# Attention, 2D FFT and a ReLU MLP on one core: the written-out order of the work made anew from the last loads of w2 on, with some of the w2 product's helper sums on GpSimd

## The chip, the core and the metric

One core of one Trainium2 chip runs the whole kernel. TensorE (PE in the profile), VectorE (DVE), ScalarE (ACT), GpSimd (POOL) and SyncE (SP) each work through their own list of instructions in order and wait on semaphores for each other and for DMAs. The metric is device time in microseconds (us), the median of the timed runs; lower is better.

## The reference

```python
scores = scale * np.matmul(q, k.transpose(0, 1, 3, 2))
...
keep = is_global | is_local          # 8 global keys, 96 local ones
...
scores = np.where(keep, scores, -1000000000.0)
a = np.exp(scores - max); a = a / (sum + 1e-09)
x = np.matmul(a, v)                  # as (4, 768, 512)
...
u = x + np.real(np.fft.fft(np.fft.fft(x, axis=1), axis=2))
un = (u - mu) / np.sqrt(var + 1e-06)
ch = np.maximum(un @ w_ch1, 0.0) @ w_ch2
return u + ch
```

There are 4 batches of 768 rows, 8 heads of 64, and a model width of 512; w_ch1 is 512 x 2048, w_ch2 is 2048 x 512. The bias of the scores falls with the distance between query and key (ALiBi), and makes most of a row's keys vanish.

## The kernel before

**Stages.** A batch goes through attention (scores, exponential on ACT, product with the mask table on DVE, product with v), is written to DRAM as xd by ACT's queue (`wr` in `bounce`, L872/L874) and read back with other rows on the partitions as xr: four sixths by SP's queue (`rd`, L884), two sixths by an indirect DMA from POOL in reversed order (`rg`, L887). The FFT uses the symmetry of the real part: DVE folds the sequence, PE multiplies with tables (py, then pu), ACT or DVE evict (zy, L1118/L1120), a reversed copy rev is made (L1139 to L1141), and DVE adds pu to xr, which gives u and its sums (L1232 to L1251). Then the rows are normed (un, L1269/L1271), turned by a DMA transpose on SP's queue into unT (L1292), and go through the MLP.

**Chunks.** The 3072 rows make 12 chunks of 256 rows, three to a batch. A chunk has eight ph units (eight matmuls of 128 x 256 each, evicted with ReLU into hT by ACT L1344 or DVE L1345) and its products with w2. Chunks 0 and 1 take eight pg units (L1370). Chunks 2 to 11 use a scheme with seven half products instead of eight: p1, p6 and p7 add up in one PSUM tile, pgA, and p4+p5 and p3+p2 in another, pgD (L1484); DVE adds them to u (L1502). The scheme needs four sums of blocks of hT for each chunk, each 128 x 1024 in fp16, made by `s_sums`: s1 (L1448) and s2 (L1454) in tiles that p45 and p6 read, s3 (L1451) in place in hT, and s4 (L1459) over s2 when p6 is done, for the product that reads it last. It needs sums of w2's blocks as well (`w2_sums`, L1420 to L1426), which DVE makes once, in two halves; the second to fourth sums overwrite w2 and so wait until the products of chunks 0 and 1 are done. All of the sums are on DVE.

**What sets the order.** `Plan` holds, for each engine, a table `ORDER` with the names of its work in the order of issue, and `run` issues each engine's next name at the time that a planner's costs give. The costs decide only how the engines' lists interleave in the program's text and which ring buffer a unit takes; each engine's own order is the table's. In the names A is an attention unit (A45 to A56 are the scores of the third batch, batch 2, A57 to A60 its products with v, A61 to A76 the same of batch 3), M a unit of the FFT or the norm, H a ph unit (H8c to H8c+7 belong to chunk c), G a product with w2 (G0 to G15 for chunks 0 and 1, G16+5(c-2) and the four after it for chunk c). A name with a dot is an operation that follows that PE unit, and T.n is one of the others: the xd writes, the sums, the transposes, the stores.

Of the kernel before, what the change touches and what calls it, by code (L numbers as in the profile page):

```python
# [12 lines left out]
ALU = mybir.AluOpType  # L13
# [11 lines left out]
class Plan:  # L25
# [9 lines left out]
    MIX = 1.3  # L35
    LANDED = {"HW": 0.55, "SW": 1.3}
    LAT = {"ACT": 0.14, "DVE": 0.12, "POOL": 0.08}
# [84 lines left out]
    def op_go(self, eng, name, start):  # L122
# [6 lines left out]
        if eng == "POOL":  # L129
            self.ports.append((start, end, 1 if dma else 0 if outs and outs[0][0] in ("vB", "kB") else 2))  # L130
        if dma:
            at = max(max(end + 0.55, 5.5) if eng == "POOL" else end + lat + 2.7 * (lat == 1.0 and end > 3.5), self.now)
# [19 lines left out]

    SHARED = {"kB": 1, "vB": 1, "sid": 1, "f1": 0, "f2": 0, "f3": 0, "z": 0, "g0": 0, "w": 0, "s": 0, "w2a": 0, "w2t": 0, "ex": 0}
# [3 lines left out]
    def beside(self, start, cost, kind):  # L157
# [4 lines left out]
        if names:  # L162
            s = self.op_start("POOL", names[-1])
            if s is not None:
                p = self.made[names[-1]]
                ports = ports + [(max(s, start), max(s, start) + p[0]["POOL"][0], 1 if p[7] else 0 if p[3] and p[3][0][0] in ("vB", "kB") else 2)]
# [15 lines left out]
    def move(self, go=False):  # L182
# [4 lines left out]
        both = [h[2] for k, h in act if k != "AQ" or sw]  # L187
        each = sum(both) * (self.MIX if len(both) > 1 else 1.0) / 1000.0
        rate = {k: h[2] / 1000.0 if k == "AQ" and not sw else each for k, h in act}
        t = min([self.now + h[1] * rate[k] for k, h in act] + [h[0] for k, h in heads if h[0] > self.now + 1e-9] + [self.NEVER])  # L190
        if not go:
            return t
# [28 lines left out]
    def unit_start(self, unit):  # L221
# [7 lines left out]
        if not there:  # L229
# [126 lines left out]
def pool(n):  # L356
    return 0.16 + n / 1080.0


@with_exitstack  # L360
def kernel(
# [156 lines left out]
    def load_v(b, hp):  # L518
        h0 = 2 * hp
        if b >= FB:  # L520
# [3 lines left out]
            swq(whole, 1.08, [("avdone", b - 2), ("wl", 7)], [("v", b, hp, t) for t in range(2)], (1536, 0.93), False)  # L524
            return
        if b == 1:
            for t in range(2 - hp % 2 * 2):
# [3 lines left out]
                swq(four, 1.08, [], [("v", b, hp, t), ("v", b, hp + 1, t)], (1536, 0.93))  # L531
            return
        for t in range(2):
# [3 lines left out]
            swq(run, 0.85, ([("avdone", b - 2), ("wl", 7)] if b > 1 else []), [("v", b, hp, t)], (768, 0.93), b < 2)  # L537
# [4 lines left out]
    def load_qk(b, hp):  # L542
# [3 lines left out]
        for w, src in enumerate((q, k)):  # L546
            if b >= FB:
                for h in range(2):
# [4 lines left out]
                    swq(run, 0.85, free(tag, ti) + [("wl", 7)], [("qk", n, w, h)], (768, 0.93), False)  # L553
# [25 lines left out]
            if n == 4:  # L579
# [5 lines left out]
                swq(two, 1.08, free(tag, ti), [("qk", n, w), ("qk", n + 1, w)], (1536, 1.53))  # L585
# [7 lines left out]
            swq(run, 0.85, free(tag, ti), [("qk", n, w)], (768, 1.53))  # L593
# [110 lines left out]
    def score(b, hp, g):  # L704
# [3 lines left out]
        def run(start, ring):  # L708
# [37 lines left out]
            e = pl.pe((0.45, 0.45, 0.34)[g] if pem else 0.24, start, "64x64" if pem else "64x32")  # L746
# [61 lines left out]
    def av(b, hp):  # L808
# [28 lines left out]
        def part(start, ring, x, k):  # L837
# [15 lines left out]
            pl.later([("DVE", 0.17 + 0.03 * m + m * dve(384), lambda: norm(po, k))], free(*XT[b]), e,  # L853
# [10 lines left out]
    def bounce(b):  # L864
# [26 lines left out]
        pl.later([("POOL", 1.1, rg)], xw + [("xr", b), ("c", "back")], 0.0, [("xg", b)], dma=(128, 4.94), rank=0)  # L891

    def fold_s(b):
# [3 lines left out]
        for n, (c0, cw) in enumerate(parts):  # L897
# [43 lines left out]
            pl.later([("DVE", (4 if b else 2) * dve2(cw), f3)], [("f2", b, n)], 0.0, [("f3", b, n)])  # L941
# [192 lines left out]
    def mirror(b):  # L1134
# [8 lines left out]
        pl.later([("POOL", 0.8, lambda: r0(nc.gpsimd.tensor_copy)), ("DVE", 0.3, lambda: r0(V.tensor_copy))], [("y", b, 0, 3), ("y", b, 3, 3)] + free("rev0", b), 0.0,  # L1143
# [286 lines left out]
    def s_sums(c):  # L1430
# [16 lines left out]
        def s1():  # L1447
            VT(new(0), block(1, 0), block(1, 1), op=ALU.add)  # L1448
# [340 lines left out]
```

## Time and profile before

| what | value |
|---|---|
| timed runs (3) | 246.86, 248.51, 248.96 us, median 248.51 |
| profiled execution, its own time | 245.87 us |
| its span, first to last instruction | 244.1 us |
| mean granted TensorE clock | 0.991 |
| DMA traffic | 32.85 MB, mean 135 GB/s |

The profile gives one execution. The page's first part is the busy time of each engine; the table by stages gives it for stretches of the span, with the number of instructions in brackets; the timeline lists instructions with their start, their length and, in brackets, the idle time ahead of them with what ended it; the chain of waits follows the end of the span back to what released each step. Matmuls overlap, so the distance from one PE unit's start to the next (its pitch) is shorter than the length that a row gives: 0.87 us for a ph unit, of which the row says 1.04.

### The profile page before, as it was taken

The page shows a single profiled execution, that of the slowest core. Times are in us where ns is not written, and L with a number is a line of the kernel's source. Part 1 is how long each engine was busy: PE and PEld are TensorE (multiplying, and loading weights), DVE is VectorE, ACT ScalarE, POOL GpSimd, SP SyncE. Part 2 cuts the span into 40 slices and gives each one's busy share as a digit, 9 for nine tenths or more (in the row PEclk, how much of TensorE's full clock was granted, in tenths as well). Part 3 has the DMA queues.
Part 4 walks back from the last instruction along what each step waited for, and adds up shares of the span by engine and source line. Part 5 has one row for each costly group of instructions (what it writes and reads, how often), then busy time and mean ns, then how long its engine had stood idle before and what let it go on. Part 6 is the DMA issues. An engine that isn't in the chain of part 4 may idle for free.

```text
span 244.1 us, 7606 instructions
## 1 busy us (share of the span) xinstructions
PE 232.0 (95%) x3251; PEld 191.2 (78%) x3251; DVE 193.4 (79%) x420; ACT 138.8 (57%) x226; POOL 114.8 (47%) x164
## 2 busy tenths in 40 slices
PE   7679899999999999999999999999999999999993
PEld 2557776878677667788989888898889898888883
DVE  2559997879972789999999889889998755846483
ACT  2368788864657468658357788364534651434200
POOL 8998898866590038999059056500300320011020
PEclk9997999999999999999999999999999999999999
DMA  6999999999999999999999979220570330040212
GB/s 170 181 169 145 157 235 172 197 190 196 110 145 152 234 179 205 117 135 110 242 184 285 135 84 156 46 33 13 174 258 4 77 99 0 1 130 1 89 72 99
DMA packets 95938, 32.85 MB, mean 135 GB/s; under 512 B 84160, under 2 KB 92480, under 8 KB 95904
## 3 DMA queue, kind: packets, MB, share of 16 engines
q0 software_dynamic: 66176, 17.06, 71.7%
q1 hardware_dynamic: 26560, 12.56, 25.1%
q10 hardware_dynamic: 3168, 2.75, 4.1%
q8 instruction: 25, 0.41, 0.7%
q14 instruction: 9, 0.07, 0.1%
HBM read 31.44 MB, written 8.65 MB: 164 GB/s over the span
## 4 chain that ended last, share of the span: by engine, by line
PE 67%; DMA 14%; DVE 5%; ACT 5%; POOL 3%; issue 3%; SPq 1%; POOLq 0%
PE ph L1339 29%; PE pgD L1484 14%; PE pgA L1484 10%; DMA qk<-in_q_dram 4%; DMA v<-in_v_dram 4%; PE py L1105 3%; DMA hT<-in_q_dram 3%; PE pg L1370 3%; PE pav L822 3%; ACT ex L766 2%; DMA back<-backm 2%; DMA xr<-xd,back 2%; PE sc L737 2%; PE pu L1192 1%; ACT mk L1657 1%
## 5 line engine op out<-in xcount | busy, mean ns | idle before, releaser
L1339 PE MATMUL ph<-unT,w 128*128 128x256 f16 x768 | 94.4, 273 | 0.8 <-issue 0.4
L1339 PEld LDWEIGHTS <-w 128*128 128x128 f16 x768 | 73.6, 98 | 12.5 <-issue 1.2
L1344 ACT ACTIVATE hT<-ph 128x512 f16<-128x512 f32 x73 | 42.9, 596 | 54.6 <-PE ph L1339 52.6
L1484 PEld LDWEIGHTS <-hT 128*128 128x128 f16 x320 | 31.0, 98 | 4.3 <-issue 0.4
L1285 POOL TENSOR_SCALAR sm<-sm 128x2 f32<-128x2 f32 x12 | 3.4, 284 | 58.2 <-ACT un L1278 57.8
L763 ACT ACTIVATE er<-sc 128x1024 f16<-128x1024 f32 (+1 forms) x24 | 22.3, 951 | 11.4 <-PE sc L737 8.2
L1345 DVE TENSOR_SCALAR hT<-ph 128x512 f16<-128x512 f32 x23 | 15.7, 687 | 12.7 <-PE ph L1339 12.7
L766 ACT ACTIVATE ex<-sc 128x1024 f16<-128x1024 f32 (+1 forms) x24 | 21.7, 955 | 7.1 <-PE sc L743 6.9
L1502 DVE SCALAR_TENSOR_TENSOR u<-pgA,sm,u 128x256 f32<-128x256 f32 (+1 forms) x30 | 16.9, 568 | 6.4 <-PE pgA L1484 6.0
L1502 DVE SCALAR_TENSOR_TENSOR u<-pgD,sm,u 128x512 f32<-128x512 f32 (+1 forms) x21 | 15.2, 722 | 3.5 <-PE pgD L1484 3.3
L1355 POOL DMA_INDIRECT out_dram<-u,back x4 | 4.5, 1120 | 27.5 <-DVE rev L1140 16.3
L887 POOL DMA_INDIRECT xr<-xd,back x3 | 4.8, 1602 | 25.4 <-PE pg L1370 16.1
L1370 PE MATMUL pg<-w,hT 128*128 128x512 f16 x64 | 16.0, 379 | 0.0
L1118 ACT ACTIVATE zy<-py 128x1024 f16<-128x1024 f32 (+1 forms) x13 | 11.1, 857 | 8.4 <-PE py L1105 6.1
L778 DVE TENSOR_TENSOR ex<-er,mk 128x1024 f16<-128x1024 f16 (+1 forms) x24 | 15.1, 646 | 0.7 <-ACT er L763 0.7
L1278 ACT ACTIVATE un<-un 128x512 f16<-128x512 f16 x24 | 15.0, 625 | 1.1 <-DMA unT<-un 1.1
L552 POOL DMA_DIRECT2D qk<-in_k_dram x16 | 13.7, 903 | 1.2 <-DMA w<-in_moe_w_ch_dram 0.8
L1269 ACT ACTIVATE un<-u,sm 128x512 f16<-128x512 f32 x19 | 13.1, 717 | 1.9 <-DVE sm L1251 0.7
L552 POOL DMA_DIRECT2D qk<-in_q_dram x16 | 13.6, 870 | 0.0
L822 PEld LDWEIGHTS <-ex 128*128 128x128 f16 x352 | 12.4, 97 | 1.1 <-ACT ex L766 0.4
L834 DVE TENSOR_TENSOR x<-pav,rc 128x384 f16<-128x384 f32 x24 | 12.6, 554 | 0.6
L822 PE MATMUL pav<-v,ex 128*128 128x65 f16 x224 | 12.9, 193 | 0.2
(170 smaller groups left out, 492.9 us busy)
## 6 DMA issues: line engine op xcount, KB each, us to landing
w<-in_moe_w_ch_dram POOLq DMA_DIRECT2D x8, 512.0 KB, 13.4
out_dram<-u SPq DMA_DIRECT2D x15, 256.0 KB, 3.0
v<-in_v_dram POOLq DMA_DIRECT2D x12, 192.0 KB, 5.8
qk<-in_k_dram POOLq DMA_DIRECT2D x16, 96.0 KB, 5.4
qk<-in_q_dram POOLq DMA_DIRECT2D x16, 96.0 KB, 4.5
xr<-xd SPq DMA_DIRECT2D x3, 512.0 KB, 4.6
xd<-x ACTq DMA_DIRECT2D x2, 768.0 KB, 4.5
v<-in_v_dram POOLq DMA_DIRECT2D x8, 96.0 KB, 7.0
```

Source lines behind the costliest of these rows:

```text
L552: nc.gpsimd.dma_start(qk16[n][:, w, :, h], src[b, h0 + h].rearrange("(i m) d -> m i d", m=P))
L763: A(mine(), cut(pa), AF.Exp, 0.0, 0.125)
L766: A(cut(expst[hp][:, :, g * 512:g * 512 + (384 if g == 2 else 512)]), cut(pa), AF.Exp, 0.0, 0.125)
L778: VT(o, mine(), m, op=ALU.mult)
L822: nc.tensor.matmul(o[:, s * 65:(s + 1) * 65], lhsT, w, start=(a == 0), stop=(a == len(ops) - 1), skip_group_check=True)
L1278: A(x, x, AF.Square, accum_out=MV[c][:, a, 2:3])
L1339: nc.tensor.matmul(ph[:, a * CH:(a + 1) * CH].rearrange("p (x m) -> p x m", x=2), W1[0][:, d, jb * P:(jb + 1) * P], UNT[c][:, :, d, :], st ...
L1344: pl.later([("ACT", act(512), lambda: A(dst, ph, AF.Relu)), ("DVE", dve(512), lambda: V.tensor_scalar_max(dst, ph, 0.0))], [], e, [("h", c ...
L1345: ("DVE", dve(512), lambda: V.tensor_scalar_max(dst, ph, 0.0))],
L1370: nc.tensor.matmul(pg, HT[c][:, jb, t * P:(t + 1) * P], W2[0][:, jb, :], start=(jb == 0), stop=(jb == NJ - 1))
L1484: nc.tensor.matmul(o, lhs(j), rhs(j), start=(first and j == 0), stop=(j == NK - 1), skip_group_check=True)
L1502: V.scalar_tensor_tensor(o, x, r(t), acc, op0=ALU.mult, op1=ALU.add)
```

## The change

The tables' beginnings are kept: on PE up to H12, the unit that starts at 57.45 us in the trace of before, on the other engines to about the same time. Behind it every table is made anew. The planner's costs are changed at many places, which acts only through what is said above of them. Three of the edits change what the engines do:

- The sums s1 to s4 of chunks 3 to 11 may stand in POOL's table as well as in DVE's (`slow`). In the new tables 14 of the 40 are on POOL: s2 and s3 of chunk 3, s4 of chunk 4, s1 of chunk 5, s1, s2, s3 of chunk 6, s2, s3, s4 of chunk 7, s1 and s3 of chunk 9, s2 of chunk 10 and s2 of chunk 11. In exchange two of the four vB copies of batch 2 and one of batch 3 (L793/L795) and batch 2's rev go from POOL to DVE, and batch 3's rev from DVE to POOL.
- PE does the same units in another order. Two score groups of batch 2 that stood behind G20 (A48, A49) stand ahead of G17, and the first product of chunk 3, G21, stands behind the last of chunk 4's ph units in the list, H39, where it stood among the first of them.
- ACT writes batch 1's xd earlier in its list, and SP's read of it stands one place earlier; SP's later stores and POOL's loads are reordered: chunk 1's rstd on POOL (M8.8), which stood ahead of eight loads of batch 2's q and k, stands behind them.

Lines below H12 move by 11 to 14 in the changed kernel (s1 is L1459, s3 L1462, s2 L1465, s4 L1470). The edits, without the planner's other costs, and one line of the tables for each of PE, DVE and POOL:

```diff
+def pool2(n):
+    return 0.2 + n / 450.0
...
-        def s1():
-            VT(new(0), block(1, 0), block(1, 1), op=ALU.add)
+        def s1(on=V):
+            on.tensor_tensor(new(0), block(1, 0), block(1, 1), op=ALU.add)
...
+        def slow(fn):
+            return [("POOL", pool2(NK * P), lambda: fn(nc.gpsimd))] if c > 2 else []
+
-        pl.later([("DVE", us, s1)], hs + sfree(0), 0.0, [("s", c, 1)], rank=1)
+        pl.later([("DVE", us, s1)] + slow(s1), hs + sfree(0), 0.0, [("s", c, 1)], rank=1)
...
-            "H26 H27 G17 A56 A50 H31 G18 A55 M20 G19 A57 H28 H30 A60 H29 G20 A48 A49 H32 H33 A59 G21 A58 H36 H38 G22 G23 H34 G24 H37 H39 G25 H35 A61 A62 "
+            "H29 G18 A53 A56 H31 H30 A54 A50 H28 G19 M20 G20 A55 A52 H24 H26 A58 H39 G21 A59 A57 G22 A60 H37 H32 G23 H38 H36 G25 G24 H33 H34 A61 A72 H35 "
...
-            "A56.1 A50.1 G18.0 M17.7 G17.0 M20.0 A55.1 T.203 A57.0 A60.0 G19.0 G20.0 T.207 T.208 A48.1 A49.1 A59.0 T.210 A58.0 G21.0 T.142 G23.0 T.209 "
+            "T.126 A56.1 T.124 A53.1 G17.0 T.123 M20.0 A50.1 G19.0 A54.1 G20.0 A52.1 T.207 A58.0 A55.1 A57.0 G21.0 A59.0 A60.0 G22.0 G23.0 T.209 T.142 "
...
-            "T.112 T.158 T.163 T.167 T.125 T.126 T.169 T.164 T.156 T.153 T.154 T.124 T.162 T.155 M17.5 T.141 M17.11 T.157 T.166 T.172 T.160 T.159 M20.5 "
+            "G15.1 T.169 T.125 T.162 T.163 T.159 M17.5 T.166 T.155 T.153 T.170 T.157 T.158 M17.11 T.208 T.210 T.141 T.164 T.165 T.160 T.156 T.215 T.174 "
```

What this does to the engines' lists is shown at three places.

**ACT, batch 1's two writes of xd.** Before, the writes (`xd<-tt`) stand on either side of the eviction of py_1, whose py is unit M16 on PE; mk<-distk are pieces of a mask table, un<-un the squares of chunk 2's norm.

```order
63 L1344 ACTIVATE hT_1538<-ph_0_1744 128x512
64 L1657 ACTIVATE mk<-distk 128x640
65 L874 DMA xd_1780<-tt_1401 64x6x512
66 L1118 ACTIVATE zy_1753<-py_1_1782 128x1024
67 L874 DMA xd_1780<-tt_1401 64x6x512
68 L1657 ACTIVATE mk<-distk 128x640 x4
69 L1344 ACTIVATE hT_1792<-ph_4_1813 128x512
```

The same place of the changed kernel:

```order
58 L1129 ACTIVATE zy_1740<-py_0_1718 128x1024
59 L1671 ACTIVATE mk<-distk 128x640
60 L885 DMA xd_1760<-tt_1411 64x6x512
61 L1671 ACTIVATE mk<-distk 128x640
62 L885 DMA xd_1760<-tt_1411 64x6x512
63 L1671 ACTIVATE mk<-distk 128x640 x2
```

The second write now waits for nothing but one piece of mk; the evictions of py_3 and py_1 have gone to DVE.

**DVE, from the w2 sums to the second sum of chunk 2.** Before, the first half of the w2 sums (L1424 to L1426) stands ahead of batch 1's u (L1244 to L1251), the second half behind it, and then the exponentials' products (ex) and chunk 2's s1 (eg) and s2 (sb).

```order
139 L1250 TENSOR_TENSOR sm_2075<-sm_2075,u_2074 128x2
140 L1251 TENSOR_SCALAR sm_2075<-sm_2075 128x2
141 L1424 TENSOR_TENSOR w_0_711<-w_0_711 128x4x256
142 L1425 TENSOR_TENSOR tt_1996<-w_0_711 128x1024
143 L1426 TENSOR_TENSOR tt_1996<-w_0_711,tt_1996 128x1024
144 L778 TENSOR_TENSOR ex_82<-er_2030,mk 128x2x384
145 L1448 TENSOR_TENSOR eg<-hT_1792 128x1024
146 L778 TENSOR_TENSOR ex_80<-er_2085,mk 128x2x512
147 L1502 SCALAR_TENSOR_TENSOR u_1249<-pgA_2065,sm_1250,u_1249 128x256
148 L1454 TENSOR_TENSOR sb<-eg,hT_1792 128x1024
```

The same place of the changed kernel, from the first half of the w2 sums to the first rows of batch 1's u:

```order
126 L1435 TENSOR_TENSOR w_0_713<-w_0_713 128x4x256
127 L1436 TENSOR_TENSOR tt_1976<-w_0_713 128x1024
128 L1437 TENSOR_TENSOR tt_1976<-w_0_713,tt_1976 128x1024
129 L1435 TENSOR_TENSOR w_0_713<-w_0_713 128x4x256
130 L1436 TENSOR_TENSOR tt_1976<-w_0_713 128x1024
131 L1437 TENSOR_TENSOR tt_1976<-w_0_713,tt_1976 128x1024
132 L1392 SCALAR_TENSOR_TENSOR u_1012<-pg_0_1825,sm_1013,u_1012 128x512
133 L1255 SCALAR_TENSOR_TENSOR u_2067,sm_2068<-pu_1904,xr_1843 128x3x128
```

Both halves of the w2 sums now stand in one block ahead of the last add of chunk 1 (u_1012) and of batch 1's u; behind u come s1, two of the ex, the add of p1 and s2, in this order.

**POOL, where the first three sums are put.** Before, between the rstd of a norm (sm, L1285/L1286) and the next, POOL only issues loads, batch 2's reversed read of xd (L887) and copies vB.

```order
116 L1286 TENSOR_TENSOR sm_1951<-sm_1951,mhalf 128x2
117 L887 DMA xr_2748<-xd_2666,back 128x1024
118 L1285 TENSOR_SCALAR sm_2075<-sm_2075 128x2
119 L1286 TENSOR_TENSOR sm_2075<-sm_2075,mhalf 128x2
120 L552 DMA qk_2284<-in_q_dram 128x6x64
121 L522 DMA v_85<-in_v_dram 128x12x64
122 L793 COPY vB_87<-v_85 128x528
```

The same place of the changed kernel, with chunk 3's s2 and s3 and chunk 4's s4:

```order
110 L1296 TENSOR_SCALAR sm_2068<-sm_2068 128x2
111 L1297 TENSOR_TENSOR sm_2068<-sm_2068,mhalf 128x2
112 L1465 TENSOR_TENSOR sb<-eg,hT_2087 128x1024
113 L1462 TENSOR_TENSOR hT_2087<-hT_2087 128x8x128
114 L898 DMA xr_2780<-xd_2691,back 128x1024
115 L563 DMA qk_2325<-in_k_dram 128x6x64 x2
116 L563 DMA qk_2345<-in_k_dram 128x6x64
117 L533 DMA v_85<-in_v_dram 128x12x64
118 L1470 TENSOR_TENSOR sb<-hT_2493,sb 128x1024
```

Three sums have come in, two of them ahead of the reversed read and of the loads for batch 3.

More of the change, by code (lines that the diff above doesn't have):

```diff
@@ L35 @@
     MIX = 1.3
+    ALONE = 1.54
     LANDED = {"HW": 0.55, "SW": 1.3}
-    LAT = {"ACT": 0.14, "DVE": 0.12, "POOL": 0.08}
+    LAT = {"ACT": 0.18, "DVE": 0.12, "POOL": 0.08}
     def __init__(self):
@@ L129, in op_go @@
         if eng == "POOL":
-            self.ports.append((start, end, 1 if dma else 0 if outs and outs[0][0] in ("vB", "kB") else 2))
+            self.ports.append((start, end, 1 if dma else 0 if outs and outs[0][0] in ("vB", "kB", "ts", "w1s", "s") else 2))
         if dma:
-            at = max(max(end + 0.55, 5.5) if eng == "POOL" else end + lat + 2.7 * (lat == 1.0 and end > 3.5), self.now)
+            at = max(max(end + 0.95, 5.33) if eng == "POOL" else end + lat + 2.7 * (lat == 1.0 and end > 3.5), self.now)
             cell = [self.NEVER]
@@ L165, in beside @@
                 p = self.made[names[-1]]
-                ports = ports + [(max(s, start), max(s, start) + p[0]["POOL"][0], 1 if p[7] else 0 if p[3] and p[3][0][0] in ("vB", "kB") else 2)]
+                ports = ports + [(max(s, start), max(s, start) + p[0]["POOL"][0], 1 if p[7] else 0 if p[3] and p[3][0][0] in ("vB", "kB", "ts", "w1s", "s") else 2)]
         for a, b, dma in ports:
@@ L186, in move @@
         sw = any(k == "SW" for k, h in act)
-        both = [h[2] for k, h in act if k != "AQ" or sw]
+        nxt = self.q["SW"][1][0] if len(self.q["SW"]) > 1 else self.NEVER
+        us = {k: h[2] * (self.ALONE if k == "SW" and h[2] < 2.0 and nxt > self.now + 1e-9 else 1.0) for k, h in act}
+        both = [us[k] for k, h in act if k != "AQ" or sw]
         each = sum(both) * (self.MIX if len(both) > 1 else 1.0) / 1000.0
@@ L190, in move @@
         t = min([self.now + h[1] * rate[k] for k, h in act] + [h[0] for k, h in heads if h[0] > self.now + 1e-9] + [self.NEVER])
+        if sw and nxt > self.now + 1e-9:
+            t = min(t, nxt)
         if not go:
@@ L344, in act @@
 def act(n):
-    return 0.1 + n / 1180.0
+    return 0.055 + n / 1180.0
 def dve(n):
@@ L890, in bounce @@
         pl.later([("SP", 0.38, rd)], xw + free("xr", b), 0.0, [("xr", b)], lat=2.0, dma=(128, 10.4))
-        pl.later([("POOL", 1.1, rg)], xw + [("xr", b), ("c", "back")], 0.0, [("xg", b)], dma=(128, 4.94), rank=0)
+        pl.later([("POOL", 1.6, rg)], xw + [("xr", b), ("c", "back")], 0.0, [("xg", b)], dma=(128, 4.94), rank=0)
     def fold_s(b):
@@ L1142, in r0 @@
             Y[(b, 0, 3, "r")], Y[(b, 3, 3, "r")] = rev[:, 0], rev[:, 1]
-        pl.later([("POOL", 0.8, lambda: r0(nc.gpsimd.tensor_copy)), ("DVE", 0.3, lambda: r0(V.tensor_copy))], [("y", b, 0, 3), ("y", b, 3, 3)] + free("rev0", b), 0.0,
+        pl.later([("POOL", 1.1, lambda: r0(nc.gpsimd.tensor_copy)), ("DVE", 0.3, lambda: r0(V.tensor_copy))], [("y", b, 0, 3), ("y", b, 3, 3)] + free("rev0", b), 0.0,
                  [("y", b, 0, 3, "r"), ("y", b, 3, 3, "r")], [("free", "zy", 2 * b + 1)])
@@ L1272, in centre @@
         for a in range(2):
-            pl.later([("ACT", 0.62, lambda a=a: un("ACT", a)), ("DVE", 1.3 if c < 2 else 0.38, lambda a=a: un("DVE", a))],
+            pl.later([("ACT", 0.62, lambda a=a: un("ACT", a)), ("DVE", 1.3 if c < 2 else 0.55, lambda a=a: un("DVE", a))],
                      [("u", c, a)] + free("un", c), 0.0, [("un", c, a)])
@@ L1286, in rstd @@
             nc.gpsimd.tensor_tensor(r, r, mhalf, op=ALU.pow)
-        pl.later([("POOL", 0.82, rstd)], [("ss", c, 0), ("ss", c, 1)], 0.0, [("rstd", c)], rank=2)
+        pl.later([("POOL", 1.25, rstd)], [("ss", c, 0), ("ss", c, 1)], 0.0, [("rstd", c)], rank=2)
     def nt_dma(c):
@@ L1357, in st @@
                                          in_=UT[c].rearrange("p r d -> p (r d)"), in_offset=None)
-        pl.later([("POOL", 1.1, st)], needs, 0.0, [], [("free", "u", c + pl.U0)] * 2, dma=(128, 11.25), rank=0)
+        pl.later([("POOL", 1.25, st)], needs, 0.0, [], [("free", "u", c + pl.U0)] * 2, dma=(128, 11.25), rank=0)
     def pg_unit(c, t, part):
@@ L1610, in dma_const @@
             ways = ways + [("POOL", 0.66, lambda: nc.gpsimd.dma_start(dst, src.ap()))]
-        pl.later(ways if soon else ways[:1], needs, 0.0, [tok], lat=1.0 if soon else 3.2, dma=us)
+        pl.later(ways if soon or tok == ("dk",) else ways[:1], needs, 0.0, [tok], lat=1.0 if soon else 3.2, dma=us)
     with tc.manual_schedule():
```

55 lines of the change are left out of this document (28 added, 27 removed), and 47 rows, old and new, of the table ORDER.

## The prediction

> **What bounds the kernel now.** I read the page first: the span, the busy time of each engine, and the first line of the chain of waits.
>
> ```profile
> span 244.1 us, 7606 instructions
> PE 232.0 (95%) x3251; PEld 191.2 (78%) x3251; DVE 193.4 (79%) x420; ACT 138.8 (57%) x226; POOL 114.8 (47%) x164
> PE 67%; DMA 14%; DVE 5%; ACT 5%; POOL 3%; issue 3%; SPq 1%; POOLq 0%
> ```
>
> PE works 232.0 of 244.1 us. The change leaves PE's units as they are and moves them, so what it can win is PE's idle time behind the point where the orders part (57.45 us). The table by stages says where that idle time is.
>
> ```profile
> core 0: us, PE busy (x) PEld busy (x) DVE busy (x) ACT busy (x) POOL busy (x), PEclk, DMA share, GB/s
> 0.00:57.50 57.50, 50.01 (x1084) 37.68 (x1085) 43.13 (x109) 39.61 (x54) 50.21 (x82) 0.97 1.63 181
> 57.50:88.00 30.50, 30.50 (x303) 20.64 (x300) 22.28 (x43) 17.11 (x31) 10.46 (x13) 1.00 1.50 174
> 88.00:106.00 18.00, 17.05 (x273) 13.77 (x272) 17.27 (x39) 14.52 (x24) 15.85 (x20) 1.00 1.50 147
> 106.00:160.00 54.00, 54.00 (x825) 47.24 (x821) 50.51 (x111) 35.02 (x57) 29.73 (x38) 1.00 1.11 150
> 160.00:231.00 71.00, 71.00 (x700) 63.95 (x698) 52.49 (x108) 32.34 (x63) 7.26 (x12) 1.00 0.26 76
> 231.00:244.10 13.10, 9.40 (x84) 7.93 (x82) 7.74 (x13) 0.17 (x1) 1.24 (x1) 0.96 0.21 80
> ```
>
> The first stage, with 7.5 us of idle PE, is kept. From 57.5 to 231 PE has no gap except 0.95 us between 88 and 106; the end's 3.7 us is the last adds and stores, whose order is nearly kept. DVE is 96% busy in that stage and 94% in the next: little can be laid on it there, and what is taken off it shows only where PE waits for it. The gaps one by one, from PE's timeline:
>
> ```profile
> 93.58 0.38 PE L1105 MATMUL py<-t,ww 128*128 128x256 f16 x2
> 94.34 1.91 PE L1339 MATMUL ph<-unT,w 128*128 128x256 f16 x16 [0.37 <-DMA unT<-un]
> 100.34 0.37 PE L737 MATMUL sc<-qkT 64*32 64x128 f16 x18
> 100.88 0.37 PE L737 MATMUL sc<-qkT 64*32 64x128 f16 x18 [0.17 <-ACT er L763]
> 104.21 0.39 PE L1192 MATMUL pu<-t,zy 128*128 128x128 f16 x4
> 104.90 1.03 PE L1484 MATMUL pgA<-misc,hT 128*128 128x256 f16 x8 [0.31 <-DVE u L1502]
> ```
>
> Matmuls overlap, so I measure a wait by starts: each unit's distance to the next less the shortest such distance of its kind. By that the three gaps are 0.53 (chunk 3's rows, unT), 0.36 and 0.17 (scores around 100.9) and 0.47 us (p7 waiting for DVE), 1.5 us together. This is the most that undoing waits can bring.
>
> **Part 1: batch 1's xd goes out earlier (gain 1.5).** What the gap at 94.34 waits for, followed back:
>
> ```profile
> 63.80 0.26 POOL L1285 TENSOR_SCALAR sm<-sm 128x2 f32<-128x2 f32 x1 [4.75 <-ACT un L1278]
> 75.74 0.58 ACTq L874 DMA_DIRECT2D xd<-tt  x1
> xd<-tt ACTq DMA_DIRECT2D x2, 384.0 KB, 6.7
> 82.21 0.52 SPq L884 DMA_DIRECT2D xr<-xd  x1
> 83.26 4.77 DMA back<-backm
> 88.94 3.98 DMA xr<-xd,back
> 89.47 1.24 SPq L1292 DMA_TRANSPOSE unT<-un  x1
> 92.95 0.87 DVE L1244 SCALAR_TENSOR_TENSOR u<-pu,xr 128x384 f32<-128x384 f32 x1 [0.41 <-DMA xr<-xd,back]
> ```
>
> The second write of xd starts at 75.74, the read xr 6.5 us later, the transposes 7.3 us after that, and DVE's second u waits for the indirect read at 92.95. In the changed list the second write waits for one piece of mk instead of the eviction behind M16: it starts at about 74.6, 1.1 earlier. POOL no longer stops 4.75 us for chunk 1's rstd ahead of eight loads, so SP's transposes ahead of xr are not late either, and the write has less beside it. I estimate xr and all behind it 1.1 to 2.4 us earlier: unT lands between 91.9 and 93.2 (94.30 in the trace), the indirect read between 90.5 and 91.8. PE reaches chunk 3's first ph at 93.5 (below). The first gap closes. The others come from DVE's list being late behind that u, and go with it.
>
> **Part 2: DVE's list between 88 and 98 (cost 0.6).** The new list puts both halves of the w2 sums ahead of u. They wait for the last product of chunk 1. In the trace:
>
> ```profile
> 86.72 0.41 PE L737 MATMUL sc<-qkT 64*32 64x256 f16 x18
> 87.06 1.04 PE L1370 MATMUL pg<-w,hT 128*128 128x512 f16 x4
> 87.93 1.04 PE L1339 MATMUL ph<-unT,w 128*128 128x256 f16 x8
> 89.13 0.69 DVE L1424 TENSOR_TENSOR w<-w 128x1024 f16<-128x1024 f16 x1
> 91.19 0.69 DVE L778 TENSOR_TENSOR ex<-er,mk 128x1024 f16<-128x1024 f16 x1
> 95.55 0.68 DVE L1424 TENSOR_TENSOR w<-w 128x1024 f16<-128x1024 f16 x1
> 97.76 0.55 DVE L778 TENSOR_TENSOR ex<-er,mk 128x768 f16<-128x768 f16 x1
> ```
>
> In the changed order the same units stand ahead of that product less one score group (0.34 by its start and the next), so it ends at 87.6. DVE starts at about 87.9 and needs 2.06 + 2.21 for the two halves (91.19 - 89.13, 97.76 - 95.55), 0.67 for an add, 2.6 for u (95.55 - 92.95), 0.6 for s1, 2 x 0.6 for two ex, 0.4 for p1's add and 0.6 for s2: 10.3, s2 at 98.2. PE has ahead of p6 of chunk 2, which reads s2, seven ph and p1 at 0.87 (the distance of the starts at 87.06 and 87.93), p45 at twice that, a py at 0.66 and four score groups at 0.4 with their switches: 11.0, so it asks at 98.6. That is no wait if no row of DVE's ten slips. In the trace such rows slip by 0.4 (at 92.95) and more, so the bounds are 0 and 1.2, and I take 0.6. This is the place to look first: the gaps of Part 1 partly come back here.
>
> **Part 3: fourteen sums on POOL (cost 0.4).** The trace has no POOL instruction with two wide inputs. The rows nearest to it, and DVE's price:
>
> ```profile
> L793 POOL COPY vB<-v 128x528 f16<-128x528 f16 x11 | 7.3, 668 | 3.4 <-DMA v<-in_v_dram 3.2 <-issue 0.2
> L683 POOL COPY mk<-qkT 128x512 f16<-128x512 f16 x7 | 4.5, 647 | 2.3 <-DVE qkT L676 1.2 <-ACT qkT L679 1.1
> L684 POOL COPY mk<-qkT 128x128 f16<-128x128 f16 x7 | 2.4, 346 | 0.4
> L1451 DVE TENSOR_TENSOR hT<-hT 128x1024 f16<-128x1024 f16 x10 | 7.5, 750 | 0.0
> L793 DVE COPY vB<-v 128x528 f16<-128x528 f16 x5 | 1.6, 312 | 1.5 <-DMA v<-in_v_dram 1.3
> ```
>
> From 128 to 512 columns a POOL copy grows by 0.301 us, 0.78 ns a column: 1.05 us for 1024 columns of one input, the lower bound. The upper bound is 4.4: the slowest copy below took 1.14 us for 528, 2.2 for 1024, twice for two inputs. I take 2 x 1.05 = 2.1, nearest to the undisturbed rows, and 0.25 for DVE getting in between, 2.35. So each moved sum ends 2.35 - 0.60 = 1.75 us later than on DVE, and costs something only where its reader is nearer. [...]
>
> The nearest readers, from the changed list and the pitches above: chunk 4's s4, made when p6 is done, has a py (0.66), p45 (1.75), a ph (0.87) and two score groups (0.6) ahead of its reader, 3.9; less 0.2 for the last matmul's end, 0.2 for two handovers and up to 0.4 for a DVE instruction in its way, 3.1: no wait at 2.35. Chunk 11's s2 has p7 and p32 of chunk 10 and p1 and p45 of its own, 5.2, less 1.7 for the eviction, s1 and handovers: 3.5, no wait. At the others the distance is larger, but chunk 5's s1 opens a chain, s2 and p45 behind it, and I put 0.3 there (bounds 0 and 1.75) and 0.1 on the end. DVE is relieved of 14 x 0.60 = 8.4 us, of which two vB copies, a third and a rev take back some 2.5; this wins nothing where PE has no gap.
>
> The two engines do hold each other up, by two pairs of rows at the same time:
>
> ```profile
> 112.14 0.62 POOL L795 COPY vB<-v 32x528 f16<-32x528 f16 x1
> 112.38 0.93 DVE L1448 TENSOR_TENSOR eg<-hT 128x1024 f16<-128x1024 f16 x1
> 131.23 0.68 DVE L1448 TENSOR_TENSOR eg<-hT 128x1024 f16<-128x1024 f16 x1
> 131.25 1.14 POOL L795 COPY vB<-v 32x528 f16<-32x528 f16 x1
> ```
>
> Where POOL began first, DVE's s1 took 0.25 longer than its 0.68; where DVE began first, POOL's copy took 0.52 longer than 0.62. Whoever starts second waits for the first. [...]
>
> **Part 4: the score groups.** From the parting on PE has 14 stretches of scores instead of 15; entering and leaving one costs about 0.1 each: -0.2.
>
> **Sum.** -1.5 (Part 1) + 0.6 (Part 2) + 0.4 (Part 3) - 0.2 (Part 4) = -0.7 us, on the profiled execution 245.87 (span 244.1, 1.8 around it) -> 245.2. That execution lies below the three timed runs (246.86, 248.51, 248.96; median 248.51). I carry the difference to the middle of the four, 247.7: **247.0 us**.
>
> **The rivals.**
> - *The waits of 93 to 105 stay away and nothing takes their place*, faster: -1.5 - 0.2 on the profile, and if the timed runs' 1 to 3 us over the profile stand in these DMA-bound gaps, as much again: 247.7 - 3.2 = 244.5. For it: the gaps hang on DMA chains, which differ between executions. Against it: DVE's list has no room (Part 2). Chance 0.20.
> - *POOL's sums hold DVE*, slower. Place: 106 to 160, where DVE has 54.00 - 50.51 = 3.5 us idle and is not relieved (four sums out, 2.4 us; copies and rev in, 2.5). Four of the sums fall there. If DVE is held for half of each, the lag is 4 x P/2 - 3.5: 1.2 us at P = 2.35, 3.5 at P = 3.5, and chunk 4's s4 itself is 0.4 late at 3.5. It decides from P of about 3, when the lag passes the 1.75 to 2.5 us that the sums are ahead of their readers. At P = 3.5: 247.7 + 3.9 - 0.7 = 250.9. For it: the pairs of rows above. [...] Chance 0.25.
> - *The change does nothing that can be measured though its waits move*: Part 2's wait comes to 1.2 and Part 3's to 1, and the sum is +0.5: 248.2. It is within the same band as my forecast, and its share of it is 0.20.
>
> **How the numbers follow.** A measurement of this kernel tells about 1% (2.5 us) from no change, the timed runs lying 2.1 apart. My forecast has 0.35, the third rival 0.20, together 0.55 within 1%; faster by over 1% is the first rival, 0.20; slower by over 1% the second, 0.25. The range reaches from the first rival's 244.5 to 251.0, the second's at P = 3.5; what is left out are prices above that, up to the bound of 4.4, and scatter below.
>
> **What would show it.** Part 1: PE has no gap at chunk 3's first ph, and xr starts before 81.2. Part 2: a gap ahead of chunk 2's p6 with DVE s2 (sb) as its releaser, at 98 to 100. Part 3: POOL rows of the sums at 2.0 to 2.6 us, and none of them the releaser of a gap over 0.5. The forecast is wrong if the mean POOL sum is over 3 us, or DVE's ex and sums between 106 and 160 grow by more than 2 us together, or the stage from 106 to 231, now without a gap, shows one over 1 us.

## The result and the profile after

The changed kernel took 250.88 us (median of 20 runs, 248.48 to 253.91), the kernel before 247.02 (20 runs, 245.16 to 249.99). The ratio is 1.0135, 95% interval 1.0103 to 1.0167: 1.35% slower, 3.3 us. Ratios here and below compare only those runs of a kernel that lie within 1.5% of its fastest (13 of the 20 here, and no more than 5 of 12 in e1), and the profiled execution of the changed kernel (252.53, span 250.8) is not one of them, so its trace shows more loss than the ratio. The prediction was 247.0 and no change. The page, in the lines that were shown of before:

```profile
span 250.8 us, 7613 instructions
PE 233.7 (93%) x3251; PEld 192.0 (77%) x3251; DVE 197.8 (79%) x418; ACT 133.4 (53%) x220; POOL 140.1 (56%) x172
PE 57%; DMA 14%; DVE 13%; ACT 5%; POOL 5%; SPq 3%; issue 2%; DVEq 0%; ACTq 0%; POOLq 0%
```

PE's work is the same; its share of the chain fell from 67 to 57%, and DVE's rose from 5 to 13%. The table by stages says where:

```profile
core 0: us, PE busy (x) PEld busy (x) DVE busy (x) ACT busy (x) POOL busy (x), PEclk, DMA share, GB/s
0.00:57.50 57.50, 48.44 (x1056) 36.37 (x1057) 41.99 (x106) 38.37 (x53) 48.80 (x81) 1.00 1.68 178
57.50:88.00 30.50, 30.40 (x305) 21.23 (x303) 22.88 (x47) 17.21 (x31) 10.56 (x15) 1.00 1.47 176
88.00:106.00 18.00, 17.93 (x278) 14.07 (x277) 17.69 (x39) 13.18 (x20) 17.59 (x21) 1.00 1.55 153
106.00:160.00 54.00, 50.53 (x745) 43.09 (x745) 47.62 (x101) 33.75 (x58) 29.28 (x31) 0.97 1.15 145
160.00:231.00 71.00, 70.38 (x737) 63.34 (x730) 56.49 (x112) 28.03 (x56) 29.32 (x24) 1.00 0.26 76
```

The 0.95 us of idle PE between 88 and 106 are gone (17.93 of 18.00 busy), as forecast. Between 106 and 160, where PE had no gap before, it idles 3.5 us, and 0.6 between 160 and 231. And 28 matmuls fewer are done by 57.5: H12 starts at 58.8 instead of 57.45. PE's timeline shows the new gap:

```profile
141.00 1.04 PE L1350 MATMUL ph<-unT,w 128*128 128x256 f16 x8
142.76 0.41 PE L748 MATMUL sc<-qkT 64*32 64x256 f16 x18 [0.73 <-ACT zy L1129]
144.90 0.37 PE L748 MATMUL sc<-qkT 64*32 64x128 f16 x18 [1.73 <-DVE u L1259]
146.13 1.34 PE L1498 MATMUL pgD<-w,sb 128*128 128x256 f16 x8 [0.86 <-DVE u L1516]
147.27 1.91 PE L1498 MATMUL pgD<-w,hT 128*128 128x256 f16 x8
148.97 1.60 PE L1498 MATMUL pgA<-misc,hT 128*128 128x256 f16 x8
```

By starts, as in the prediction, five units in a row lose 0.89, 1.91, 1.05, 1.10 and 0.56: 5.5 us. Only the first three, 3.85 us, are waits. The last two, 1.66 us, have no idle time ahead of them; their matmuls are slower (1.34 to 1.91 us in the rows, 1.04 elsewhere), because the granted clock was 0.50 from 146.70 to 150.11. The column behind the five busy times, ahead of the DMA share, is that clock:

```profile
141.00:146.70 5.70, 2.39 (x52) 1.81 (x50) 3.92 (x17) 5.05 (x8) 2.12 (x5) 1.00 0.69 99
146.70:150.11 3.41, 3.41 (x19) 2.35 (x17) 3.41 (x4) 0.73 (x3) 3.27 (x3) 0.50 0.60 115
150.11:153.00 2.89, 2.89 (x44) 2.34 (x43) 2.84 (x6) 1.02 (x1) 2.62 (x3) 1.00 0.18 11
```

So the gap has two parts, waits and a slower stretch right behind them. DVE, which PE waits for there, over the same time:

```profile
138.97 2.07 DVE L1247 TENSOR_SCALAR sm<-sm 128x2 f32<-128x2 f32 x1
142.72 0.87 DVE L1255 SCALAR_TENSOR_TENSOR u<-pu,xr 128x384 f32<-128x384 f32 x1 [1.68 <-DMA out_dram<-u]
146.38 3.07 DVE L789 TENSOR_TENSOR ex<-er,mk 128x1024 f16<-128x1024 f16 x2
```

Two things stand out. An instruction on 128 x 2 elements, 0.17 us elsewhere, took 2.07, and two ex took 3.07 instead of 1.3. And DVE waited for a store, `out_dram<-u`, before it could write batch 2's second u. POOL's sums at the same time, and their price:

```profile
138.90 2.11 POOL L1470 TENSOR_TENSOR sb<-hT,sb 128x1024 f16<-128x1024 f16 x1 [7.45 <-PE pgA L1498]
146.78 2.25 POOL L1459 TENSOR_TENSOR eg<-hT 128x1024 f16<-128x1024 f16 x1 [1.76 <-ACT hT L1355]
```

The store is followed back in the chain of waits; its columns are start, length and what:

```profile
129.24 2.19 SPq L642
131.53 3.07 SPq L642
134.69 7.95 DMA out_dram<-u
```

There are four u buffers, so chunk 7's u (the rows that L1255 writes) goes into chunk 3's. It must wait until the last of chunk 3's stores (T.211) has landed. In SP's list that store now stands behind two transposes of batch 3, which wait for loads; it leaves at 134.69, takes 7.95 us, and DVE starts at 142.72. The trace of before shows the same pair, two rows that the prediction did not read (SP's queue, then DVE):

```profile
132.60 0.34 SPq L1603 DMA_DIRECT2D out_dram<-u  x1
```

```profile
137.46 0.87 DVE L1244 SCALAR_TENSOR_TENSOR u<-pu,xr 128x384 f32<-128x384 f32 x1 [0.44 <-DMA out_dram<-u]
```

There DVE already waited 0.44 us for that store, hidden from PE: the buffer had no slack, and nothing but this small idle time said so. In the changed kernel u starts 5.3 us later (142.72 against 137.46). The store's later start is 2.1 us of that (134.69 against 132.60), 1.36 of them the later H12; the other 3.2 us are a longer transfer, 7.95 us where before took 4.7. What makes the transfer longer was not tried.

### The profile page after: what moved, and what is told of

It is laid out like the page before. It is cut to its first block, busy times and chain, and to the rows that moved or that the text cites. A ratio compares the mean times of both kernels' runs of the same rounds, so it can differ in the third digit from the quotient of the medians.

```text
span 250.8 us, 7613 instructions
## 1 busy us (share of the span) xinstructions
PE 233.7 (93%) x3251; PEld 192.0 (77%) x3251; DVE 197.8 (79%) x418; ACT 133.4 (53%) x220; POOL 140.1 (56%) x172
## 4 chain that ended last, share of the span: by engine, by line
PE 57%; DMA 14%; DVE 13%; ACT 5%; POOL 5%; SPq 3%; issue 2%; DVEq 0%; ACTq 0%; POOLq 0%
PE ph L1350 22%; PE pgD L1498 12%; PE pgA L1498 8%; DMA w<-in_moe_w_ch_dram 6%; DMA v<-in_v_dram 5%; PE pg L1381 4%; ACT ex L777 3%; DMA out_dram<-u 3%; PE pz L1660 2%; PE pav L833 2%; SPq L642 2%; PE pu L1203 2%; PE py L1116 2%; DVE ex L789 2%; DVE u L1255 1%
## 5 line engine op out<-in xcount | busy, mean ns | idle before, releaser
L1498 PEld LDWEIGHTS <-hT 128*128 128x128 f16 x320 | 31.7, 100 | 5.0 <-issue 0.3
L1356 DVE TENSOR_SCALAR hT<-ph 128x512 f16<-128x512 f32 x24 | 16.4, 686 | 8.9 <-PE ph L1350 8.6
L789 DVE TENSOR_TENSOR ex<-er,mk 128x1024 f16<-128x1024 f16 (+1 forms) x24 | 17.2, 734 | 1.0 <-ACT er L774 1.0
L1381 PE MATMUL pg<-w,hT 128*128 128x512 f16 x64 | 15.4, 379 | 0.1
L898 POOL DMA_INDIRECT xr<-xd,back x3 | 3.4, 1118 | 21.7 <-PE pg L1381 7.9
L1131 DVE CAST zy<-py 128x512 f16<-128x512 f32 (+1 forms) x11 | 9.0, 831 | 3.9 <-ACT zy L1129 2.1
L1465 POOL TENSOR_TENSOR mk<-mk,hT 128x1024 f16<-128x1024 f16 x2 | 4.3, 2126 | 13.2 <-DVE mk L1459 13.2
```

The costliest lines, as they stand in the source:

```text
L789: VT(o, mine(), m, op=ALU.mult)
L1356: ("DVE", dve(512), lambda: V.tensor_scalar_max(dst, ph, 0.0))],
L1381: nc.tensor.matmul(pg, HT[c][:, jb, t * P:(t + 1) * P], W2[0][:, jb, :], start=(jb == 0), stop=(jb == NJ - 1))
L1498: nc.tensor.matmul(o, lhs(j), rhs(j), start=(first and j == 0), stop=(j == NK - 1), skip_group_check=True)
```

## The experiments

Three causes were open. **Theory U** (S in the first expectations): the late store keeps the u buffer. **Theory H**: a sum on POOL keeps DVE out while it lasts (a hold, below). **Theory F**: the 1.36 us in front of H12 have a cause in the changed kernel. The rival to all is that the new order is worse in itself (Q). Each kernel was timed against the kernel before on the same chip; "stretch" is the time from H12's start to the last product unit's in its profile, 181.9 us before and 187.2 in the changed kernel, which leaves the front (all ahead of H12) out. The last column is by starts; in brackets is the part of it that lies in a stretch of 3.41 us with a granted clock of 0.50.

| kernel | ratio to before, 95% interval | stretch, us | PE gaps, us |
|---|---|---|---|
| changed | 1.0135, 1.0103 to 1.0167 | 187.2 | 5.5 (1.7) at 141 to 151, 0.95 at 193 to 196 |
| e1, all 14 sums on DVE | 1.0053, 1.0011 to 1.0095 | 185.0 | 3.1 at 142 to 146 |
| e2, four sums on DVE | 1.0131, 1.0091 to 1.0170 | 187.3 | 5.8 (1.6) at 142 to 151 |
| e3, store early in SP's list | 1.0177, 1.0146 to 1.0208 | 187.5 | 4.5 (1.6) at 143 to 151, 0.95 at 195 |
| e12, add early in DVE's list | 1.0177, 1.0125 to 1.0228 | 187.9 | 4.3 (1.3) at 143 to 148, 0.95 at 194 |
| e6, add and store early | 1.0053, 1.0019 to 1.0087 | 182.2 | 0.95 at 188 |
| e9, e6 and one sum on DVE | 1.0002, 0.9971 to 1.0033 | 181.5 | 1.1 at 99 |
| e4, store early, four sums on DVE | 1.0080, 1.0049 to 1.0111 | 185.1 | 1.8 at 143, 1.35 at 151 |
| e7, e6, four sums on DVE, constant back | 1.0028, 0.9990 to 1.0066 | 183.1 | 1.4 at 148 |
| e11, e6 and all 14 sums on DVE | 1.0008, 0.9969 to 1.0048 | 183.2 | 1.5 at 142, 0.6 at 150, 0.5 at 236 |
| e5, one planner constant back | 1.0102, 1.0044 to 1.0160 | 184.5 | 2.6 at 142 to 145, 0.95 at 192 |
| e8, before with the 14 sums on POOL | 1.0276, 1.0224 to 1.0329 | 187.7 | 0.6 at 121, 2.7 at 148 to 151, 1.8 at 186 |
| e10, before again | 1.0010, 0.9980 to 1.0040 | 182.0 | as before |

**e1, all 14 sums back on DVE**, each behind a name of DVE's table at which its inputs are ready; the piece with chunk 4's s4 (T.215) and chunk 5's s1 (T.218):

```diff
-A62.1 A72.1 M23.0 M23.6 G27.0 G28.0 A70.1 A63.1 G30.0
+A62.1 A72.1 M23.0 T.215 M23.6 G27.0 G28.0 A70.1 A63.1 T.218 G30.0
```

> All 14 sums back on DVE, next to where their inputs are ready; the rest of the new order kept. Theory H (a sum on POOL keeps DVE out for its whole 2.1 us): the three long DVE rows beside POOL sums (2.07, 2.47, 2.03 us) go back to 0.2 to 0.7, the PE gaps between 141 and 151 shrink from 5.5 us to about 2, the one at 193 (0.95) goes: 2 to 4 us faster than the changed kernel, within 0.5% of before. Theory S (the late store of chunk 3's u, which DVE's u of batch 2 waits for, is the cost): the gap of 141 to 146 stays, under 1.5 us faster than the changed kernel. Theory Q (the new order itself is worse, with or without POOL): no faster than the changed kernel.

The long DVE rows and the gap at 193 are gone, but 3.1 us stay: u still waits for the store (2.56 us of DVE idle time, to 142.63). The stretch is 2.2 us shorter, but 1.7 of that is the slow clock, which this trace does not have: of the waits alone, 3.85 us in the changed kernel, only 0.75 went. The ratio is as expected, 1.0053, but the twelve runs lie between 248.08 and 254.97 us with a median of 251.91 (248.20 for before), so it is weak evidence of a gain.

**e2, four sums on DVE**: the ones beside which a DVE row was long (chunk 4's s4, chunk 5's s1, chunk 7's s4, chunk 9's s1), placed as in e1.

> Only the four sums beside which a DVE row was long go back to DVE (chunk 4's s4, chunk 5's s1, chunk 7's s4, chunk 9's s1); ten stay on POOL. Theory H: as with all 14 on DVE, within 0.5 us, as the other ten held nothing up. If where a hold falls is chance from run to run, the ten others hold DVE elsewhere and the gain is under half of that. Theory S: under 1.5 us faster than the changed kernel.

DVE from 140, and then SP's queue:

```profile
140.15 0.17 DVE L1247 TENSOR_SCALAR sm<-sm 128x2 f32<-128x2 f32 x1
143.53 0.85 DVE L1255 SCALAR_TENSOR_TENSOR u<-pu,xr 128x384 f32<-128x384 f32 x1 [2.62 <-issue]
```

```profile
130.11 4.76 SPq L642 DMA_TRANSPOSE qkT<-qk  x2
135.09 0.62 SPq L1617 DMA_DIRECT2D out_dram<-u  x1
```

The hold is gone (0.17 again), u starts no earlier (143.53, as the store that leaves at 135.09 takes 8.4 us), and the gap is as large as in the changed kernel. So H does not set the gap of 141 to 151: behind the hold stood the store, and taking away the nearer wait alone gives nothing.

**e3, the store early.** Chunk 3's store (T.211) ahead of the read of xd (T.140) and the transposes:

```diff
-T.205 T.206 T.140 T.179 T.182 T.211 T.149
+T.205 T.206 T.211 T.140 T.179 T.182 T.149
```

> Only SP's list: the store of chunk 3's first u rows stands ahead of batch 2's read of xd and two transposes instead of behind them. Theory S: DVE's u of batch 2 starts at once, 2 to 3 us faster than the changed kernel. Theory H: u starts when the hold by chunk 4's s4 ends, 1.5 us earlier than now at most, so 0.5 to 1.5 us faster. Theory Q: same.

```profile
129.30 5.92 SPq L1617 DMA_DIRECT2D out_dram<-u  x4
135.32 1.30 SPq L895 DMA_DIRECT2D xr<-xd  x1
```

A miss on every theory's number, and a lesson: the store's data comes from an add (G25.0) that stands late in DVE's list, at 134.1. SP stopped at the store until then, and the read of xd behind it left at 135.3 instead of 128.8. u now waited for that (DVE idle 3.81 us). So this run does not test theory S.

**e12, the add early.** PE is done with chunk 3's pgD at about 123.5, but its add stood behind the folding for the FFT and chunk 4's s1:

```diff
-T.145 G24.0 T.146 A61.1 T.147 T.213 G25.0 G26.0
+T.145 G25.0 G24.0 T.146 A61.1 T.147 T.213 G26.0
```

> The changed kernel with only the add of chunk 3's first u rows early on DVE; SP's list as in the changed kernel, the store behind two transposes. If SP's list holds the store (it left at 134.7 in the changed kernel although its add ended at 132.9): it leaves at 134 to 135 all the same, the gap of 141 to 146 stays, ratio to before 1.010 to 1.016. If the add held it: the gap goes as with both edits, ratio 1.003 to 1.008.

The add ends at 128; the store does not move, as it stands behind the transposes in SP's list, and the gap stays, as expected if SP's list holds the store (the ratio is a little above the range named, with an interval that covers it). DVE's row, and the two of SP:

```profile
142.89 0.84 DVE L1255 SCALAR_TENSOR_TENSOR u<-pu,xr 128x384 f32<-128x384 f32 x1 [3.40 <-DMA out_dram<-u]
```

```profile
130.60 4.71 SPq L642 DMA_TRANSPOSE qkT<-qk  x2
135.36 0.62 SPq L1617 DMA_DIRECT2D out_dram<-u  x1
```

**e6, both**: e12's edit, and the store behind the read of xd and ahead of the transposes.

> The changed kernel with DVE's last add of chunk 3's first u rows five places earlier in its list (right ahead of the other rows' add) and its store on SP ahead of two transposes. Theory U (batch 2's second u waits until the store of chunk 3 has left its buffer): that store starts at about 129 instead of 134.7, u no longer waits for it, and 1.5 to 2 us of the 5.5 between 141 and 151 go: 1.2 to 2.2 us faster than the changed kernel; the 2.07 us hold by chunk 4's s4 stays. Rival (the hold alone sets the gap): under 0.5 us.

```profile
128.69 0.43 SPq L1617 DMA_DIRECT2D out_dram<-u  x1
```

```profile
137.50 0.88 DVE L1255 SCALAR_TENSOR_TENSOR u<-pu,xr 128x384 f32<-128x384 f32 x1
```

The store leaves six us earlier, u starts at 137.5 without a wait, and all 5.5 us go, the slow clock with them, although chunk 4's s4 is still on POOL: DVE has passed the small instruction by then, and the sum, which starts at 137.90, takes 0.6 us from the rows behind it instead of 1.9 ahead of u. Ratio 1.0053. e12 differs from this only in the store's place in SP's list and kept a gap of 4.3 us (ratio 1.0177), and e3 has the early place without the early add. So theory U is shown, with both lists as its cause.

**e9, e6 and chunk 7's s4 on DVE.** The one hold that still cost PE time, in the changed kernel: DVE's row, POOL's, ACT's, and PE's three units around the gap.

```profile
192.20 2.03 DVE L1247 TENSOR_SCALAR sm<-sm 128x2 f32<-128x2 f32 x1
```

```profile
192.09 2.12 POOL L1470 TENSOR_TENSOR sb<-hT,sb 128x1024 f16<-128x1024 f16 x1 [2.36 <-PE pgA L1498]
```

```profile
194.32 1.33 ACT L1280 ACTIVATE un<-u,sm 128x512 f16<-128x512 f32 x2 [8.35 <-DVE sm L1247]
```

```profile
193.50 1.04 PE L1350 MATMUL ph<-unT,w 128*128 128x256 f16 x8
194.67 1.03 PE L1498 MATMUL pgA<-misc,hT 128*128 128x256 f16 x8
196.19 1.03 PE L1350 MATMUL ph<-unT,w 128*128 128x256 f16 x8 [0.49 <-ACT hT L1355]
```

The hold reaches PE by two ways. DVE's add of pgA, which the second unit waits for, stood behind the small instruction (0.30 us by starts); and ACT's norm (un) waited for the small instruction's result, so that the eviction behind it in ACT's list, which the third unit waits for, was late (0.65 us).

> The early add and store as before, and one of the 14 sums, chunk 7's s4, back on DVE; 13 stay on POOL. Theory H with U: the gap of 0.95 us behind the hold at 192 (DVE's 0.17 us instruction took 2.03) goes and nothing else changes: 0.9 us faster than with the early add and store alone, the stretch from H12 to the last unit at 181.2 to 181.5 us in the profile (before 181.9), a ratio to before of 0.998 to 1.003. If the time that is left over is in the front (before H12): the stretch is as short as that and the ratio still over 1.003.

The gap is gone, and the ratio is 1.0002. Its interval (0.9971 to 1.0033) overlaps that of e6 (1.0019 to 1.0087), so what this one sum is worth rests on the trace, 0.95 us. With the two edits of U and this one of H the new order is as fast as the old; 13 sums are still on POOL. What is left in its trace is the wait of the prediction's Part 2, at chunk 2's p6:

```profile
100.76 1.05 PE L1498 MATMUL pgA<-tt,sb 128*128 128x256 f16 x8 [0.90 <-DVE sb L1465]
```

**e4** (e2 and e3 together) and **e7** (e6, e2 and the constant of e5) lie between:

> Both: four sums back on DVE and the store first. Theories H and S together: all gaps of 141 to 151 go but the stage's switches, 4 to 5.5 us faster than the changed kernel, so 0 to 1 us faster than before. If the gap has a third cause behind the two, 2 to 3 us faster than the changed kernel.

> All three undone at once: the planner constant back, the four sums beside which DVE was held on DVE, the add and the store early; ten sums stay on POOL and the new order stays. If F, H and U are the whole loss: 5 to 7 us faster than the changed kernel in the profile (gaps 1.3 + 5.5 + 0.95), so 1 to 2 us faster than before (ratio 0.992 to 0.997). If there is another cause: slower than before still.

In e4 the read of xd is late, as in e3. In e7 the gap at 148 is a wait for a transpose of batch 3's k and q, `[1.20 <-DMA qkT<-qk]`, which e4 shows at 151 too; what made the transpose late there was not tried. Both came out slower than expected.

**e11, e6 with no sum on POOL:**

> The early add and store, and all 14 sums on DVE: the new order without any POOL sum and without the wait for the buffer. If the sums on POOL win something by relieving DVE, it is slower than with 13 of them on POOL, by 0.5 to 1.5 us, with PE gaps where DVE is late (148 to 152, the tail). If they only cost: as fast or faster.

Ratio 1.0008 against e9's 1.0002: the 13 sums on POOL win nothing that can be measured, though the stretch is 1.7 us shorter with them in one profile each. Part of that is that chunk 4's s4 stands ahead of u in DVE's list here (0.69 us), and u started at 140.10 where e9 has 138.69.

**e5, the planner's constant.** In the front the built programs differ in one place: two evictions of batch 0's py, one on ACT and one on DVE, write the same zy tile, and the price of an ACT instruction decides which of them stands first in the program and which waits.

```diff
-    return 0.055 + n / 1180.0
+    return 0.1 + n / 1180.0
```

> The changed kernel with one planner constant put back (the price of an ACT instruction, 0.1 instead of 0.055 us of fixed cost). All five tables stay as they are; in the built program only one pair changes: ACT's and DVE's second evictions of batch 0's py write the same zy tile, and which of them waits for the other. Theory F (in the changed kernel DVE waits 2.13 us there for ACT's eviction, and PE 2.31 behind it): PE starts H12 at 57.3 to 57.8 instead of 58.6 to 59.6, and the kernel is 1.0 to 1.8 us faster than the changed one. Rival (the front's 1.3 us is chance between executions): no difference.

DVE's wait fell from 2.13 to 0.89 us, but PE waited 1.98 us at the same unit (2.31 in the changed kernel) and H12 started at 59.46. Theory F falls by the first of these. H12's start alone would not show it, as in this trace the granted clock was 0.50 from 42.35 to 45.76, right behind that wait. The ratio, 1.0102, has an interval that overlaps the changed kernel's. And this trace, with every sum still on POOL and no slow clock behind the gap, has waits of 2.6 us at 142 to 145, less than e1 with no sum there (3.1): one more sign that the holds do not make that gap.

**e10, before again:**

> The kernel before, unchanged, as one more kernel beside itself: how wide chance is. If the front's start of H12 (57.45 in the trace of before, 57.8 to 59.6 in seven traces of the changed order) is chance, it lies between 57 and 59.5 here too; if the changed kernel's front is slower by a cause, below 57.8. The ratio to itself should be within 0.3% of 1.

PE's row of H12 in this execution:

```profile
59.77 1.04 PE L1339 MATMUL ph<-unT,w 128*128 128x256 f16 x8
```

57.45 in the first trace of before, 59.77 here, with the same program: the front moves by more than 2 us from execution to execution, and the 1.36 of the changed kernel's trace need no cause. The ratio to itself is 1.0010. DVE's wait for the store of chunk 3 is longer here too, and PE still has no gap behind it:

```profile
140.49 0.86 DVE L1244 SCALAR_TENSOR_TENSOR u<-pu,xr 128x384 f32<-128x384 f32 x1 [1.11 <-DMA out_dram<-u]
```

So in the order before, at least 1.1 us of this wait are hidden.

**e8, the sums alone.** The tables of before, with the 14 sums moved to POOL where their inputs are ready. The planner's costs are those of the changed kernel, so the text also interleaves the lists differently:

```diff
-"M17.5 T.141 M17.11 T.157 T.166 T.172 T.160 T.159 M20.5"
+"M17.5 T.208 T.210 T.141 M17.11 T.157 T.166 T.172 T.160 T.159 T.215 M20.5"
```

> The order of before with the same 14 sums moved to POOL and nothing else (placed where their inputs are ready). Theory H: POOL rows of 2.1 us, DVE held for up to 1.9 us beside some of them, and readers that are near (chunk 5's s1, chunk 11's s2) wait: 1 to 4 us slower than before, with PE gaps of 0.5 to 2 us next to the sums. Rival (sums on POOL cost nothing by themselves, the order does): within 0.4% of before.

2.76% slower, 6.8 us, where 1 to 4 were expected. Rows of DVE, and of POOL at the time of the last two:

```profile
145.43 4.64 DVE L788 TENSOR_TENSOR ex<-er,mk 128x768 f16<-128x768 f16 x2
183.87 2.10 DVE L1087 TENSOR_TENSOR ww<-eA 128x256 f16<-128x256 f16 x1
185.89 2.20 DVE L1088 TENSOR_TENSOR ww<-eA 128x256 f16<-128x256 f16 x1
```

```profile
183.13 2.69 POOL L1464 TENSOR_TENSOR sb<-eg,hT 128x1024 f16<-128x1024 f16 x1 [3.10 <-DVE eg L1458]
185.78 2.16 POOL L1461 TENSOR_TENSOR hT<-hT 128x1024 f16<-128x1024 f16 x1
```

Two instructions of 0.28 us take 2.1 and 2.2 beside two sums, and PE waits 1.64 us for the second. The two ex at 145.43 take 4.64 us where 1.15 is usual, and the largest gap, 2.7 us up to 151, stands behind them; the second began ahead of the sum, while POOL was issuing a load, and why it was held from then on was not tried. Summed over the DVE rows that overlap a sum, each less the shortest of its kind, DVE lost about 13 us in this kernel, 7 in the changed one and 4 in e9. What a sum on POOL cost here was thus decided by what DVE had next.

## Why the prediction was wrong, point by point

- **Part 1 was right.** The second write of xd starts at 73.61 (75.74 before), the read xr at 81.15, just inside the sign of 81.2. The gap at chunk 3's first ph and the three behind it are gone; PE is busy 17.93 of 18.00 us from 88 to 106. A small one is new right behind, 0.39 us by starts, at 106.16. That PE reached chunk 3's first ph later (95.03, before 94.34) is not the reason: in e6, with H12 at 57.82, the gap is gone as well.
- **Part 2 was right in place, and in size within its bounds.** p6 of chunk 2 waits for DVE's s2: 0.1 us by starts in the changed kernel's trace, 0.1 to 0.5 in the others of this order, 1.07 in e9, where 0.6 was taken with bounds of 0 and 1.2.
- **Part 3's price was right**: the sums took 2.11 to 2.25 us, 2.35 was taken. That the readers do not wait at this price held too in the changed kernel's trace.
- **The second rival had the right effect and the wrong size.** DVE is held by sums, but not for half of each: 4 of the 14 took 1.9, 1.9, 1.9 and 0.6 us from DVE, each from an instruction with all operands in SBUF, the other ten 0.7 together. Of these only the one at 192 is shown to cost PE time by itself, 0.95 us. That the rival's 250.9 us is so near to the measured 250.88 is luck: it priced a sum at 3.5 us, the sums took 2.11 to 2.25, and most of the loss is the store's. Its point of decision, a price of about 3 us, was wrong: at 2.1 it already costs, where the instruction that DVE has next is one that PE waits for.
- **The step that failed is the one that was not taken**: "From 57.5 to 231 PE has no gap" was read as if no list had a tight place there. The change moved chunk 3's products, batch 2's u and SP's store against each other, and the prediction priced no move on SP behind the xd read, nor the four u buffers. The row that would have shown it, DVE's wait of 0.44 us for `out_dram<-u` at 137.46, was in the trace. So the sum has no term for the store of chunk 3's u, and no reason is given for leaving it out. What it would have had to be is about 2 us by the ratios of the changed kernel and e6 (1.0135 - 1.0053 = 0.8%), and 5.5 us in the changed kernel's profiled execution: 3.85 of waits and 1.66 of the halved clock behind them, which the prediction did not have either. Why the ratios show less than the profiles stays open; e1 and e5 have no such clock behind the gap, so it is not in every execution. The last sentence on what would prove the forecast wrong, a gap over 1 us from 106 to 231, is what happened.
- **The sum of the rest fits, no more.** Taking out the store's wait and one hold leaves the new order at 1.0002 of before; the interval, 0.9971 to 1.0033, holds both no change and the forecast's -0.3%. Part 4's 0.2 us is too small to be seen.

## What to carry to other kernels

Where a program is reordered, go through the buffers that are reused and ask of each what frees it and how long the next writer already waits; a wait of 0.4 us on an engine that is not the bound says that the buffer has no slack: here u's start moved by the 2.1 us of the store's later start and the 3.2 of its longer transfer. In the order before 1.1 us of the wait stayed hidden, and DVE's waits of 1.7 to 3.4 us in the new order became PE's gap. A wait that is removed may have another of the same length behind it, so edits are tried in pairs: here two moves of which neither helped alone gave 2 us together. Before a gap is put down to waits alone, read the granted clock behind it: a clock of 0.50 made 1.66 of the 5.5 us here. Price an instruction that is moved to GpSimd by what VectorE has to do while it runs and not by its own length alone: of the 14 sums here, all of 2.11 to 2.25 us, four took 0.6 to 1.9 us each from VectorE and the other ten 0.7 together.

## What the runs showed of the hardware

A GpSimd sum of two fp16 operands of 128 x 1024 took 2.11 to 2.13 us in 13 of the changed kernel's 14 rows and 2.25 in the other; in e8 up to 2.69. While one ran, VectorE's tensor_scalar on 128 x 2 fp32 in SBUF took up to 2.07 us (0.17 in e2, at the same place without a sum) and, in the changed kernel, its tensor_tensor on fp16 in SBUF up to 2.5 (0.68), while its instructions with an operand in PSUM ran at their usual length beside other sums (x<-pav at 0.55 to 0.56 us beside the two sums of 115 to 120, 0.55 ahead of them). By these rows the instruction on two columns lost 1.9 us and the one on a thousand 1.8 to 1.9.

TensorE's granted clock fell to 0.50 for 3.41 us at the end of the gap in four traces: of the changed kernel (146.70 to 150.11), e2, e3 and e12 (from 106 to 160 us each of the four has a mean of 0.97), with 2.8 to 4.2 us of waits by starts there. Units of eight matmuls with a pitch of 0.87 us then took up to 1.70, which cost 1.3 to 1.7 us in each. Behind the gaps of e1 (3.1 us), e5 (2.6) and e4 (1.8) the clock stayed at 1.00, so the length of the waits alone does not tell which trace will show it.
